# Routing in two groups of 13 and 11 tiles, expert 0 in two chunks, and logits of three tiles side by side: a WKV attention with a mixture of experts on one core

## The chip, the core and the metric

The kernel runs on one core of one Trainium2 chip. The metric is the time of one execution in device microseconds. Three runs of the kernel before gave 615.57 to 617.15, with a median of 616.31 us. The profile shows one further execution; it has five engines: PE (TensorE, with PEld for its weight loads), DVE (VectorE), ACT (ScalarE), POOL (GpSimd) and SP (SyncE, which here issues most of the DMAs).

## The reference

A linear attention with decay (WKV) over 4 batches of 8 heads with 768 tokens of 48 dimensions, then a mixture of 8 experts over its 3072 rows of 384 values. Each row goes to the two experts with the largest noisy logits.

```python
# r, k, v: [4, 8, 768, 48]; w, u: [8, 48]
for t in range(S):
    kt, vt, rt = (k[:, :, t], v[:, :, t], r[:, :, t])
    cur = np.einsum('bhd,bhe->bhde', u[None] * kt, vt)
    y[:, :, t] = np.einsum('bhd,bhde->bhe', rt, state + cur)
    state = w[None, :, :, None] * state + np.einsum('bhd,bhe->bhde', kt, vt)
...
x = np.ascontiguousarray(attn_out.transpose(0, 2, 1, 3)).reshape(B * S, H * D)
...
logits = x @ w_gate                              # [3072, 8]
noise_scale = np.log1p(np.exp(x @ w_noise))
noisy_logits = logits + noise_scale * noise
top2 = np.argpartition(-noisy_logits, 2, axis=1)[:, :2]
...
for e in range(E):
    for k in range(2):
        mask = top2[:, k] == e
        ...
        h = np.maximum(x[mask] @ w1[e], 0.0)     # w1: [8, 384, 1024]
        out[mask] += top2_w[mask, k, None] * (h @ w2[e])
```

## The kernel before

The order of the work is written out by hand: the instructions of each engine run in the order in which the code emits them.

*Attention.* The 24 steps of the loop `for i in range(NT)` take a tile of 128 tokens each. In the trace a step is, on PE: four transposes of r (`trans(i+1, 0)`, L394), the logits of tile i-2 (L497), four transposes of k, kvup (L422, the product of keys and values for the state), inter (L447, the part of y from the state, in four quarters of the array), intra (L459, the part of y within the tile), the scores of the next tile (L406), three transposes of x(i-1) (L485) and four of y (L468). DVE makes rT from the transposed r (L399), the masked scores am (L413), the sum x of a tile (L473), and c (L377), a reduction of the product rku of r, k and u that POOL makes four times with a multiplication and once with an addition (L372). cv (L381), c times v, is on DVE up to tile 9 and on ACT (L388) after that. The decayed state z is two operations on DVE and POOL (L432, L433). SP loads r, k and v four tiles ahead, and weights of expert 0 (`w_load`, L316) into staging buffers; between them it stores each x to the DRAM tensor `xd` (L477), from which the experts gather their rows. DVE and ACT split the loaded weights into a high and a low part (L337, L332).

*Routing.* The logits of a tile are three matmuls with the transposed x as weights and the gate's columns, repeated six times, as the moving side. The tiles are routed in GROUPS of 9, 7 and 8. When a group's logits are there, its generator `route` joins a queue, and `rstep(us)`, called at fixed places of the loop, emits as many of its DVE operations as fit into that many us. They compute the noise scale and the noisy logits for the whole group (elements are tiles x 8 experts), MAX8 and its search for each tile (L709, L715), the two gates, one-hot choices om, a rank for each token by matmuls with a triangle of ones (L739), and with `drop` a list of the rows of an expert by matmuls of two factors r_oa and r_ob (L594). `one(g, 1)` is that list for expert 1, and `half` for the rest. GR (L787) holds the rows to gather. `GEARLY` is the number of groups that the first gather waits for: with groups 0 and 1 (16 tiles) routed, the first EARLY = 512 rows of expert 0 are sure.

*Experts.* Expert e is done in chunks of 128-row tiles; tile 6 has 64 rows. `xgather` issues an indirect DMA per tile on POOL (L954). `xT` transposes a gathered tile on PE (ptm, L1016), ACT copies it (xh, L1018) and DVE makes its low part (xl, L1019). `p1` (L1040) is the first product, 72 matmuls of the chunk's width in eight f of nine, with its eviction on ACT and DVE (L1042, L1044); `p2` (L1074, and L1065 and L1067 for the half tile) the second, 24 matmuls of 384 columns per tile. The result is weighted and scattered into `out` by POOL (L1095). Before that, `out` is zeroed in 16 stores of 288 KB (`zero_out`, SP, L1232), issued while the first chunk runs. Expert 0 has three chunks of 2, 2 and 3.5 tiles, the others two.

## Time and profile before

| | |
|---|---|
| median of three runs | 616.31 us (615.57 to 617.15) |
| the profiled execution | 620.86 us, its span 619.0 us |
| PE busy | 583.0 us (94% of the span) |
| PEld busy | 550.1 us (89%) |
| DVE busy | 375.8 us (61%) |
| ACT busy | 241.9 us (39%) |
| POOL busy | 278.7 us (45%) |
| TensorE's mean granted clock | 0.991 of full speed |
| DMA | 86.03 MB, mean 139 GB/s |

The profiled execution is 4.55 us longer than the median, and 1.86 us of its time lie outside the span. A row of a timeline gives the start and the duration of a run of like instructions; matmuls are pipelined, so a group's pitch (start to start) is what counts and its duration is somewhat longer. Where an engine stood idle before a row, the time and what ended it stand in brackets. On PE, fp32 matmuls are shown in two passes, so the counts in the trace are twice those in the code.

### The profile page before, as it was taken

Reading aid. Unit: us, or ns where it says so; the run is one execution under the profiler, and the core shown is the slowest. Engines: PE = TensorE matmul, PEld = TensorE weight load, DVE = VectorE, ACT = ScalarE, POOL = GpSimd, SP = SyncE. Lnnn points to the kernel's source line nnn. Section 1 sums busy time; section 2 is a strip of 40 time slices with the busy share of each in tenths; the row PEclk is TensorE's granted clock in tenths of the full one; section 3 lists DMA queues with packets and bytes.
Section 4 is the critical chain, followed back from the end, with each engine's and each line's share of the span. In section 5 each row is a group of like instructions: output and inputs, shape, how many; then the busy total and the mean of one; then the engine's idle time right before and its main releaser. Section 6 shows DMA issues by size and latency. Waiting matters only on the chain.

```text
span 619.0 us, 12834 instructions
## 1 busy us (share of the span) xinstructions
PE 583.0 (94%) x4566; PEld 550.1 (89%) x4567; DVE 375.8 (61%) x1006; ACT 241.9 (39%) x596; POOL 278.7 (45%) x428
## 2 busy tenths in 40 slices
...
GB/s 130 184 207 154 192 159 99 171 112 34 177 209 138 142 113 196 75 177 98 225 102 169 144 156 156 116 211 109 158 136 162 138 123 182 133 160 119 40 23 30
DMA packets 134556, 86.03 MB, mean 139 GB/s; under 512 B 109953, under 2 KB 124609, under 8 KB 134482
## 3 DMA queue, kind: packets, MB, share of 16 engines
...
q14 instruction: 36, 0.29, 0.2%
...
## 4 chain that ended last, share of the span: by engine, by line
PE 77%; DVE 10%; DMA 3%; SPq 2%; issue 2%; ACT 1%; another core or an unknown queue 1%; POOL 0%; POOLq 0%; DVEq 0%; ACTq 0%
PE ph L1040 32%; PE pym L1074 31%; PE pa L406 3%; DMA xd<-x 2%; DVE am L413 2%; SPq L135 2%; PE yt L459 1%; PE pym L1065 1%; PE pym L1067 1%; PE pl L497 1%; PE pt L394 1%; PE ptx L485 1%; PE ptb L468 1%; DVE rT L399 1%
## 5 line engine op out<-in xcount | busy, mean ns | idle before, releaser
L1074 PE MATMUL pym<-w1h,hb 128*128 128x384 f32 x768 | 200.2, 337 | 0.9 <-ACT hb L1042 0.7
L1074 PEld LDWEIGHTS pym<-w1h,hb 128*128 128x128 f32 x768 | 138.9, 188 | 3.8 <-issue 2.0
L1040 PE MATMUL ph<-xh,w0h 128*128 128x384 f32 (+3 forms) x408 | 138.2, 339 | 1.5 <-issue 0.9
L1040 PE MATMUL ph<-xl,w0h 128*128 128x384 f32 (+3 forms) x408 | 137.2, 336 | 0.0
L1040 PE MATMUL ph<-xh,w0l 128*128 128x384 f32 (+3 forms) x408 | 136.9, 336 | 0.0
L1044 DVE SCALAR_TENSOR_TENSOR hb<-ph,hb 128x384 fp32r<-128x384 f32 (+1 forms) x136 | 72.4, 533 | 102.2 <-ACT hb L1042 52.5
L1074 PE MATMUL pym<-w1l,hb 128*128 128x384 f32 x384 | 129.2, 337 | 0.4 <-issue 0.4
L1095 POOL DMA_INDIRECT out_dram<-ot,TK x54 | 54.7, 1013 | 151.9 <-DVE ot L1091 122.7
L1042 ACT ACTIVATE hb<-ph 128x384 fp32r<-128x384 f32 (+1 forms) x136 | 64.3, 473 | 111.7 <-PE ph L1040 82.7
L1040 PEld LDWEIGHTS ph<-xh,w0h 128*128 128x128 f32 x408 | 76.6, 188 | 4.0 <-issue 1.1
L1040 PEld LDWEIGHTS ph<-xh,w0l 128*128 128x128 f32 x408 | 76.7, 188 | 1.8
L1040 PEld LDWEIGHTS ph<-xl,w0h 128*128 128x128 f32 x408 | 76.6, 188 | 1.5
L954 POOL DMA_INDIRECT xgt<-xd,GR x40 | 40.4, 1011 | 73.3 <-DMA xq<-xgt 26.6
L1074 PEld LDWEIGHTS pym<-w1l,hb 128*128 128x128 f32 x384 | 72.1, 188 | 0.9 <-issue 0.7
L963 POOL DMA_INDIRECT pv<-out_dram,GA x47 | 51.4, 1093 | 26.4 <-issue 15.0
L1080 ACT ACTIVATE ot<-pym 128x384 f32<-128x384 f32 x39 | 19.2, 492 | 87.2 <-PE pym L1074 68.5
L1019 DVE TENSOR_TENSOR xl<-xq,xh 128x384 fp32r<-128x384 f32 (+1 forms) x40 | 21.5, 539 | 38.1 <-ACT xh L1018 25.2
L413 DVE TENSOR_TENSOR am<-pa,mneg 128x512 int32<-128x512 int32 x48 | 32.7, 683 | 14.5 <-PE pa L406 14.5
L406 PE MATMUL pa<-rT,kT 64*128 64x128 f32 x384 | 27.9, 284 | 10.3 <-DVE rT L399 8.1
L406 PEld LDWEIGHTS pa<-rT,kT 64*128 64x128 f32 x384 | 23.6, 187 | 15.1 <-issue 9.6
L954 POOL DMA_INDIRECT xg<-xd,GR x14 | 14.0, 998 | 48.7 <-DVE f L796 33.5
L362 POOL TENSOR_TENSOR kd<-kt,tabk 128x192 f32<-128x192 f32 x46 | 30.3, 680 | 9.2 <-DMA kt<-in_k_dram 8.6
...
## 6 DMA issues: line engine op xcount, KB each, us to landing
...
xq<-xgt SPq DMA_DIRECT2D x160, 36.0 KB
...
```

Of the source, the lines that this page charges most:

```text
L362: (eng or nc.gpsimd).tensor_mul(kd[i % 3][:, h, :D], kt[i][:, h], tabk[:, h, :D])
L406: nc.tensor.matmul(pa[s][:, p, :], kT[i][s * 64:(s + 1) * 64, p, :], rT[i][s * 64:(s + 1) * 64, p, :], start=True, stop=True)
L413: nc.vector.tensor_tensor(AM[i][:, s].bitcast(I32), PA[i][s].bitcast(I32), mneg.to_broadcast([128, NP, 128]), op=ALU.bitwise_and)
L954: nc.gpsimd.indirect_dma_start(out=xg[:n], out_offset=None, in_=xd[:GROUPS[GEARLY - 1][1] * 128] if early_ else xd, in_offset=bass.Indirec ...
L963: nc.gpsimd.indirect_dma_start(out=pv[:n], out_offset=None, in_=out, in_offset=bass.IndirectOffsetOnAxis(ap=GA[:n, e * NJ + t:e * NJ + t + ...
L1019: nc.vector.tensor_sub(xl[:, g], v, xh[:, g].bitcast(F32))
L1040: nc.tensor.matmul(ph[:, :w_], a[:, d, fs], x[:, :w_ // 32, d], start=(j == 0), stop=(j == len(q) - 1))
L1042: nc.scalar.activation(h_[:, f, 0, :], ph[:, a:b], AF.Relu)
L1044: nc.vector.scalar_tensor_tensor(h_[:, f, 1, :], ph[:, a:b], 0.0, h_[:, f, 0, :].bitcast(F32), op0=ALU.max, op1=ALU.subtract)
L1074: nc.tensor.matmul(py, hb[:, f, a, hs], x[:, f, :], start=(j == 0), stop=(j == len(q) - 1))
L1080: nc.scalar.activation(ot, py, AF.Copy, **({} if e else dict(scale=GT[:, t:t + 1])))
L1095: st = nc.gpsimd.indirect_dma_start(out=out, out_offset=bass.IndirectOffsetOnAxis(ap=TK[:n, q:q + 1], axis=0), in_=ot[:n], in_offset=None, ...
```

## The change

What it does, by engine and place:

- Routing in two groups of 13 and 11 tiles instead of 9, 7 and 8. The first gather now waits for the first 13 tiles and takes 3 tiles of expert 0 (EARLY = 384) instead of 4. The second group is routed during expert 0's first chunk, and expert 1's lists of the first groups, which were made in the attention loop, are made in expert 0's second chunk.
- Expert 0 runs in two chunks of 3 and 3.5 tiles.
- Logits: the transposed x of three tiles are kept (xT has three buffers), and then 9 matmuls put the gate's columns (padded to 32) as weights at three column positions of the array, with 128 columns of x moving. The result has 16 rows for each tile; ACT copies it (ys), PE transposes it back and ACT copies the three tiles' logits at once (`logits_b`, behind kvup).
- Top two: a maximum over the group's 8 columns, compared and weighted with a falling index to pick the first of equals, once more with the winner pushed down by BIG; 13 operations a group.
- For tiles up to 13, POOL's addition in rku is left out (DVE's c reduces 384 elements instead of 192) and the decay's second product is on DVE. cv is on ACT from tile 2 on. rT stands ahead of c in DVE's queue.
- The steps of the loop leave DVE's slots other lengths (STEPS_*, two lines of the table below). The zero row doubles as the source of the warming matmuls; a weight load for expert 1 moves from the second chunk of expert 0 into its first.

The lines left out are the moves of scratch tiles and the renumbered chunks.

```diff
@@ -25,25 +25,25 @@
-STEPS_A = (2.0, 2.2)
+STEPS_A = 1.3
 CV_AT = 5
-STEPS_KV = 0.4
+STEPS_KV = 0.35
...
-STEPS_P1 = 0.75
-STEPS_P2 = 3.9
+STEPS_P1 = 0.85
+STEPS_P2 = 1.1
...
-LREP = 6
-X02_AT = (4, 4, 5, 5)
+CV_DVE = 1
+POOL_LATE = 13
+BIG = 3.0e38
...
@@ -77,19 +77,19 @@
-    CHUNKS0 = ((0, 1), (2, 3), (4, 5, 6))
     CHUNKS1 = ((0, 1, 2), (3, 4, 5, 6))
     CHUNKS2 = ((0, 1, 2), (3, 4, 5))
...
-    EARLY = 512
+    EARLY = 384
...
-    GROUPS = ((0, 9), (9, 16), (16, 24))
-    GEARLY = 2
+    GROUPS = ((0, 13), (13, 24))
+    GEARLY = 1
+    LB = 3
     GB = max(b - a for a, b in GROUPS)
...
@@ -369,19 +367,20 @@
-        nc.gpsimd.tensor_add(rku[:, :, :D // 2], rku[:, :, :D // 2], rku[:, :, D // 2:])
+        if i > POOL_LATE:
+            nc.gpsimd.tensor_add(rku[:, :, :D // 2], rku[:, :, :D // 2], rku[:, :, D // 2:])
...
-        nc.vector.tensor_reduce(c8, RKU[i][:, :, :D // 2], AX.X, ALU.add)
+        nc.vector.tensor_reduce(c8, RKU[i][:, :, :D // 2 if i > POOL_LATE else D], AX.X, ALU.add)
         C8[i] = c8
-        if i <= GROUPS[0][1]:
+        if i <= CV_DVE:
...
     def uterm_c(i, a, b):
-        if i > GROUPS[0][1]:
+        if i > CV_DVE:
...
@@ -430,7 +429,7 @@
             zt = att.tile([128, NP, D], F32, name="zt", bufs=1)
             nc.vector.tensor_add(zt, kvp, Z[b][:, :, :D])
-            nc.gpsimd.tensor_mul(Z[b][:, :, :D], zt, wv)
+            (nc.gpsimd if i > POOL_LATE else nc.vector).tensor_mul(Z[b][:, :, :D], zt, wv)
...
@@ -483,29 +482,46 @@
-        t = att_pool[0].tile([128, ND, 128], F32, name="xT", bufs=1)
+        t = att_pool[0].tile([128, ND, 128], F32, name="xT", bufs=LB)
         nc.scalar.activation(t, pt, AF.Copy)
...
     def logits(i):
         g = [i >= a for a, _ in GROUPS].count(True) - 1
         j = i - GROUPS[g][0]
         if j == 0:
             LG[g] = att_pool[0].tile([128, GB, 2 * E], F32, name="lg")
-        pl = psum.tile([128, LREP, 2 * E], F32, name="pl", tag="py0")
+        if j % LB < LB - 1 and i + 1 < GROUPS[g][1]:
+            return
+        m = j % LB + 1
+        pl = psum.tile([128, 2, 128], F32, name="pl", tag="py0")
         for d in range(ND):
-            nc.tensor.matmul(pl, XT[i][:, d, :], wg[:, d, None, :].to_broadcast([128, LREP, 2 * E]),
-                             start=(d == 0), stop=(d == ND - 1))
-        nc.scalar.activation(LG[g][:, j, :], pl[:, 0, :], AF.Copy)
-
+            for a in range(m):
+                nc.tensor.matmul(pl[32 * a:32 * a + 32, 0, :], wg[:, d, :], XT[i - m + 1 + a][:, d, :],
+                                 start=(d == 0), stop=(d == ND - 1), skip_group_check=True)
+        ys = att_pool[0].tile([128, 128], F32, name="ys", bufs=1)
+        nc.scalar.activation(ys[:32 * m], pl[:32 * m, 0, :], AF.Copy)
+        PL[i] = pl, ys, m
+
+    def logits_b(i):
+        if i not in PL:
+            return
+        pl, ys, m = PL.pop(i)
+        g = [i >= a for a, _ in GROUPS].count(True) - 1
+        j = i - GROUPS[g][0]
+        nc.tensor.transpose(pl[:, 1, :32 * m], ys[:32 * m], ident[:32 * m, :32 * m])
+        nc.scalar.activation(LG[g][:, j - m + 1:j + 1, :],
+                             pl[:, 1, :32 * m].rearrange("p (a b) -> p a b", b=32)[:, :, :2 * E], AF.Copy)
...
@@ -698,30 +713,38 @@
-        yield
-        m8 = T("m8")
-        i8 = T("i8", dt=U32)
-        for j in range(n):
-            nc.vector.max(out=m8[:, j, :], in_=nl[:, j, :])
-            if j % 2:
-                yield
-        da, e2 = P(0, (128, n)) if inp else T("da", [128, n]), T("e2", [128, n])
-        nc.vector.tensor_sub(da, m8[:, :, 0], m8[:, :, 1])
-        for j in range(n):
-            nc.vector.max_index(out=i8[:, j, :], in_max=m8[:, j, :], in_values=nl[:, j, :])
-            yield 0.24
-        nc.vector.tensor_scalar(da, da, 87.0, None, op0=ALU.min)
-        ex = expneg(da, [128, n], "r2", e2, (lambda k: P(k, (128, n))) if inp else None)
-        next(ex)
...
-        nc.vector.tensor_tensor(oh, i8[:, :, 0:2].rearrange("p j k -> p k j")[:, :, :, None].to_broadcast([128, 2, n, E]),
-                                ieu[:, None, None, :].to_broadcast([128, 2, n, E]), op=ALU.is_equal)
+        mx, tb = T("mx", [128, 2, n, 1]), ier[:, None, :].to_broadcast(sh)
+        for kk in range(2):
+            nc.vector.tensor_reduce(mx[:, kk], nl, AX.X, ALU.max)
+            yield
+            q1, ix = P(1 + kk), P(2 - 2 * kk)[:, :, 0:1]
+            nc.vector.tensor_tensor(q1, nl, mx[:, kk].to_broadcast(sh), op=ALU.is_equal)
+            yield
+            nc.vector.tensor_mul(q1, q1, tb)
+            yield
+            nc.vector.tensor_reduce(ix, q1, AX.X, ALU.max)
+            yield
+            nc.vector.tensor_tensor(oh[:, kk], tb, ix.to_broadcast(sh), op=ALU.is_equal)
+            yield
+            if kk == 0:
+                n2 = P(1)
+                nc.vector.scalar_tensor_tensor(n2, oh[:, 0], -BIG, nl, op0=ALU.mult, op1=ALU.add)
+                nl = n2
+                yield
+        da, e2 = P(0, (128, n)), T("e2", [128, n])
+        nc.vector.tensor_sub(da, mx[:, 0, :, 0], mx[:, 1, :, 0])
+        yield
+        nc.vector.tensor_scalar(da, da, 87.0, None, op0=ALU.min)
+        ex = expneg(da, [128, n], "r2", e2, lambda k: P(k, (128, n)))
+        next(ex)
+        yield
...
@@ -1151,40 +1173,36 @@
     def early():
         rows(0, EARLY // 128)
         xgather(0, 0, True)
-        xgather(0, 1, True)
...
     def route_when_done(i):
         for g, (a, b) in enumerate(GROUPS):
             if b == i + 1:
-                while g == GEARLY and route_q:
-                    rstep(1)
                 push(route(g))
-                if g == 0:
-                    push(one(0, 1))
...
         if nxt:
+            trans(i + 1, 0)
             uterm_b(i + 1)
-            trans(i + 1, 0)
         if i > 1:
             logits(i - 2)
-            route_when_done(i - 2)
         if nxt:
             trans(i + 1, 1)
         kvup(i)
+        if i > 1:
+            logits_b(i - 2)
+            route_when_done(i - 2)
         inter(i)
...
-        rstep(STEPS_A[i > GROUPS[1][1]], False)
+        rstep(STEPS_A, False)
...
             early()
-            push(one(1, 1))
...
@@ -1223,8 +1241,9 @@
     xtrans(NT - 1)
     next(p1a)
     logits(NT - 1)
+    next(p1a)
+    logits_b(NT - 1)
     route_when_done(NT - 1)
-    gap[0] = 2
...
@@ -1234,37 +1253,37 @@
     for j, _ in enumerate(p1a):
-        if j == XT_AT_0:
-            for _ in xT(0, 1):
-                pass
         zero_out()
         rstep(STEPS_P1)
-    for t in p2(0, 0, zero_out):
+
+    done = [False]
+
+    def routes_done():
+        if not route_q and not done[0]:
+            done[0] = True
+            rows(EARLY // 128, NJ)
+            xgather(0, 1)
+            tokens(0, NJ)
+
+    def step00():
+        zero_out()
         rstep(STEPS_P2)
+        routes_done()
+
+    wl = w_p2(0, 0)
+    next(wl)
+    for t in p2(0, 0, step00):
+        next(wl, None)
         hold.append((0, t))
...
     while route_q:
         rstep(1)
-    if not done:
-        routes_done()
+    routes_done()
```

How this moves the instructions is shown at three places. In the names, am is the masked scores, x the tile's output, c the reduced rku, z the state.

On DVE, step 1 of attention, before:

```order
L377 TENSOR_REDUCE c_361<-rku 128x8
L381 TENSOR_TENSOR cv<-vd_92,c_361 128x384
L399 TENSOR_TENSOR rT<-pt,pwr 128x512
L435 TENSOR_TENSOR z_187<-pwarm,w_159 128x4x48
L413 TENSOR_TENSOR am<-pa,mneg 128x512
L473 TENSOR_TENSOR x<-ptb,cv 128x384
```

and now:

```order
L398 TENSOR_TENSOR rT<-pt,pwr 128x512
L376 TENSOR_REDUCE c_362<-rku 128x8
L434 TENSOR_TENSOR z_188<-pwarm,w_160 128x4x48
L412 TENSOR_TENSOR am<-pa,mneg 128x512
L472 TENSOR_TENSOR x<-ptb,cv 128x384
```

rT, which the next scores on PE wait for, moved ahead of c, and cv left DVE.

On PE, from the scores of attention's step 6 to intra of step 7, before (pl is the logits, pt the transposes of r and k, pwarm kvup, yt inter and intra):

```order
L406 MATMUL pa<-rT,kT 128x128 x8
L485 MATMUL ptx<-ident,x 128x128 x3
L468 MATMUL ptb<-ident,yb 128x128 x4
L394 MATMUL pt<-ident,rd_86 128x128 x4
L497 MATMUL pl<-wg,xT 128x96 x3
L394 MATMUL pt<-ident,kd_85 128x128 x4
L422 MATMUL pwarm<-vd_93,kd_84 48x48 x8
L447 MATMUL yt<-rT,z_189 64x128 x8
L459 MATMUL yt<-am,vd_93 64x128 x8
```

and now, from the same scores:

```order
L405 MATMUL pa<-rT,kT 128x128 x8
L484 MATMUL ptx<-ident,x 128x128 x3
L467 MATMUL ptb<-ident,yb 128x128 x4
L393 MATMUL pt<-ident,rd_86 128x128 x4
L502 MATMUL pl<-xT,wg 32x128 x9
L393 MATMUL pt<-ident,kd_85 128x128 x4
L421 MATMUL pwarm<-vd_93,kd_84 48x48 x8
L514 MATMUL pl<-ident,ys 128x96
L446 MATMUL yt<-rT,z_190 64x128 x8
L458 MATMUL yt<-am,vd_93 64x128 x8
```

Every third step has nine matmuls of logits and, between kvup and inter, the transpose of their copy ys; the other steps have neither.

On PE, the transposes ptm of expert 0's second chunk, before, in the middle of the first chunk's first product:

```order
L1040 MATMUL ph<-xh,w0h_711 128x256
L1040 MATMUL ph<-xl,w0h_711 128x256
L1040 MATMUL ph<-xh,w0l_712 128x256
L1016 MATMUL ptm<-ident,xg 128x128 x6
L1040 MATMUL ph<-xh,w0h_711 128x256
```

and now, at the end of the first chunk's second product:

```order
L610 LDWEIGHTS r_oa
L610 MATMUL pwarm<-r_ob,r_oa 128x14
L1039 MATMUL ptm<-ident,xg 128x128 x9
L1039 MATMUL ptm<-ident,xg 128x64 x3
L1063 MATMUL ph<-xh,w0h_728 128x448
L1063 MATMUL ph<-xl,w0h_728 128x448
L1063 MATMUL ph<-xh,w0l_729 128x448
```

They stand directly behind the last list matmuls (L610), and the first product of the second chunk follows on them.

## Rows read from the trace of the kernel before

**Rows 1.** The page, part 4: shares of the chain that ended last, by engine.

```profile
PE 77%; DVE 10%; DMA 3%; SPq 2%; issue 2%; ACT 1%; another core or an unknown queue 1%; POOL 0%; POOLq 0%; DVEq 0%; ACTq 0%
```

**Rows 2.** Timeline of PE: start, us, operation, tiles, shapes, count [idle before <-releaser].

```profile
160.72 0.37 PE L1040 MATMUL ph<-xh,w0h 128*128 128x256 f32 x1
...
228.21 0.34 PE L1040 MATMUL ph<-xh,w0h 128*128 128x384 f32 x1
...
229.08 0.33 PE L1040 MATMUL ph<-xh,w0l 128*128 128x384 f32 x1
...
257.89 0.36 PE L1040 MATMUL ph<-xh,w0h 128*128 128x448 f32 x1
```

**Rows 3.** Windows: bounds, length, each engine busy (count), PEclk, DMA share, GB/s.

```profile
12.00:14.00 2.00, 2.00 (x25) 1.67 (x25) 0.17 (x1) 0.60 (x1) 2.00 (x4) 0.50 1.35 180
...
30.00:40.00 10.00, 10.00 (x151) 8.84 (x150) 6.43 (x14) 4.03 (x11) 9.15 (x16) 1.00 1.05 224
...
258.00:608.00 350.00, 349.53 (x1951) 341.74 (x1950) 175.28 (x347) 129.59 (x268) 131.05 (x169) 1.00 0.50 137
```

**Rows 4.** Timeline of DVE: x of steps 9, 13 and 22.

```profile
72.82 0.56 DVE L473 TENSOR_TENSOR x<-ptb,cv 128x384 f32<-128x384 f32 x1 [1.47 <-DMA xd<-x]
...
99.55 0.56 DVE L473 TENSOR_TENSOR x<-ptb,cv 128x384 f32<-128x384 f32 x1 [0.28 <-PE ptb L468]
...
155.48 0.56 DVE L473 TENSOR_TENSOR x<-ptb,cv 128x384 f32<-128x384 f32 x1 [0.23 <-PE ptb L468]
```

**Rows 5.** Timeline of DVE: the reduction c of tile 1.

```profile
14.97 0.35 DVE L377 TENSOR_REDUCE c<-rku 128x8 f32<-128x192 f32 x1 [2.80 <-POOL rku L372]
```

**Rows 6.** Timeline of PE: first transposes, scores of tiles 1 and 2.

```profile
11.40 1.09 PE L394 MATMUL pt<-ident,rd 128*128 128x128 f32 x4 [2.22 <-DMA rd<-in_r_dram]
...
17.00 1.16 PE L406 MATMUL pa<-rT,kT 64*128 64x128 f32 x16 [1.72 <-DVE rT L399]
...
21.94 1.16 PE L406 MATMUL pa<-rT,kT 64*128 64x128 f32 x16 [0.93 <-DVE rT L399]
```

**Rows 7.** Timeline of PE: parts of steps 12 and 13 of attention.

```profile
88.48 0.56 PE L422 MATMUL pwarm<-vd,kd 128*48 128x48 f32 x16
88.97 0.67 PE L447 MATMUL yt<-rT,z 48*64 48x128 f32 x16
89.57 1.09 PE L459 MATMUL yt<-am,vd 128*64 128x128 f32 x16
...
93.18 0.60 PE L468 MATMUL ptb<-ident,yb 128*128 128x128 f32 x4
...
94.06 0.84 PE L497 MATMUL pl<-wg,xT 128*128 128x96 f32 x6
94.74 0.60 PE L394 MATMUL pt<-ident,kd 128*128 128x128 f32 x4
```

**Rows 8.** Timeline of DVE: routing of group 0 in steps 11 and 12.

```profile
86.03 1.02 DVE L699 SCALAR_TENSOR_TENSOR r_q<-r_q,prt 128x72 f32<-128x72 f32 x4
...
88.83 0.68 DVE L413 TENSOR_TENSOR am<-pa,mneg 128x512 int32<-128x512 int32 x1
89.43 1.00 DVE L337 TENSOR_TENSOR w1l<-stg,w1h 128x768 fp32r<-128x768 f32 x1
90.35 0.36 DVE L709 MAX8 r_m<-r_nl 128x8 f32<-128x8 f32 x4
```

**Rows 9.** Timeline of DVE and POOL: GR, first and last early gather.

```profile
152.79 0.17 DVE L787 TENSOR_SCALAR GR<-lt 128x4 int32<-128x4 f32 x1
...
153.25 1.16 POOL L954 DMA_INDIRECT xg<-xd,GR  x1 [7.63 <-DMA xd<-x]
...
157.24 0.95 POOL L954 DMA_INDIRECT xg<-xd,GR  x1 [0.30 <-issue]
```

**Rows 10.** Windows (as rows 3), behind the last scatter.

```profile
612.00:613.00 1.00, 0.00 (x0) 0.00 (x0) 0.00 (x0) 0.00 (x0) 0.00 (x0) 0.50 0.05 15
```

**Rows 11.** Timeline of POOL: the last scatter of the kernel.

```profile
609.59 0.98 POOL L1095 DMA_INDIRECT out_dram<-ot,TK  x1 [3.10 <-DVE ot L1091]
```

119 lines of the change are left out of this document (48 added, 71 removed).

## The prediction

> **What bounds the kernel now.** I read the chain of the work that ended last first: TensorE has 77% of it and VectorE 10% [rows 1], so every step has to be costed on TensorE, with VectorE second. The rows of TensorE in the experts' part then give three marks [rows 2]: the first expert matmul of expert 0 starts at 160.72, expert 1's first chunk at 228.21, its second chunk at 257.89. From 258 to 608 TensorE is busy 349.53 of 350 us [rows 3], and the change leaves that stretch as it is. So the change is worth as much as it moves 257.89. I cut what lies before it into attention (to 160.72), expert 0 (67.49 us to 228.21) and the first chunk of expert 1 (29.68 us, same work before and after).
>
> In attention the start of x, the output of a step's tile, marks the pace [rows 4]. Steps 0 to 5 wait in two places. VectorE stands 2.80 us for GpSimd's rku before the reduction c of tile 1 [rows 5], and because c and cv stand ahead of rT in its queue, TensorE's scores wait for rT: 1.72 and 0.93 us in the first two steps [rows 6], and little after. The DMA engines are full there, too: a share of 1.05 from 30 to 40 us [rows 3]. Steps 5 to 9 are a loop through SyncE: the store of x stands behind a weight load that waits for its staging buffer, and x of the next step but one waits for that store to land (VectorE stands 1.47 us for it ahead of x of step 9 [rows 4]). From x of step 9 to that of step 22 it is 82.66 us (72.82 to 155.48), and there VectorE is full: the routing of the first two groups lies between its attention work without a gap [rows 8]. TensorE's own work of a step is far smaller. From the rows of one step [rows 7]: kvup 0.49 (88.48 to 88.97), inter 0.60 (88.97 to 89.57), intra 1.02 (1.09 less the 0.07 by which such a group outlasts its pitch), eight transposes 0.88 (93.18 to 94.06), so 0.44 for four and 0.38 for the three of x with a start, logits 0.68 (94.06 to 94.74), and 1.09 for the scores, whose group is 1.16 [rows 6]. That is 5.6 us with logits and 4.9 without.
>
> **Attention, part by part.** *Start.* The scores of tile 1 now wait neither for c nor cv, since rT stands first. The transposes that rT needs are done by about 14; what is left is rT after the other work of TensorE, so the scores start at about 15.3 instead of 17.00: 1.7 us. The wait of 0.93 goes as well: 2.6, and a little more with the small ones behind it. The reductions over 384 instead of 192 elements (about +0.2 each) and the decay product on VectorE (+0.3, by the 0.35 of c over 192 elements [rows 5]) are covered by the cv, an operation over 384 elements, that moves to ScalarE. The DMA engines being full to 40 us, I take 3.2 us at most at step 9 and nothing more from steps 5 to 9, whose loop through SyncE the change does not touch. Bounds: 0 (the loads set the pace and the loop swallows the gain) and 4.2.
>
> *Steps 9 to 13.* Group 0's routing starts only after 13 tiles, so VectorE has here only its attention work: two masks, the low part of a weight, x, c, rT and the two of the decay, some 4.2 us a step by my estimate. TensorE sets the pace: 4.9 plus a little, say 5.0, and one step of three has the new logits. Their price is the first unknown. 9 matmuls are 18 passes. If the three column tiles run one after another, a pass costs the 0.113 us of today's logits pass (0.68 over 6 [rows 7]): 2.03. If they run side by side as well as the four tiles of inter do (0.0375 a pass), 0.68. Nearest is intra, which has two column tiles and the same 128 columns, at 0.064 a pass; for three tiles I scale to 0.042 and take 0.75. To this come the transpose back (0.11) and the wait for ScalarE's copy ahead of it: inter waits behind it, and there is 0.93 us of other work to cover a copy that queues behind kT's 0.6; I take 0.45, from 0 to 0.9. Together 1.3 us in steps 10, 13, 14, 17, 20. Steps 9 to 13 then take 4 x 5.0 + 2 x 1.3 + 0.3 = 22.9 instead of 26.73 us (72.82 to 99.55): 3.8 won.
>
> The Trainium skill speaks against this piece: TensorEngine Tiling (Array Packing), section Key Properties, says that a change of the tiling mode (not just of the tile) drains TensorE. Here kvup, inter and intra follow each other at their plain pitch [rows 7], so this trace shows no drain to speak of. By that rule two more changes a piece, each at most the 0.16 us by which a group of logits outlasts its pitch (0.84 less 0.68), would cost 0.3 x 5 = 1.6 us, and the forecast would be 615.0.
>
> *Steps 13 to 22.* Routing of 13 tiles goes into VectorE's slots of steps 14 to 22. Its operations are 104 elements instead of 72; four of 72 take 1.02 us [rows 8]. The top two now are 13 operations on the whole group, where each tile had MAX8 (four in 0.36) [rows 8] and a search that I take for a little longer: 24 tiles at 0.24 are 5.8 us, the new ones at about 0.22 are 2 x 2.9: neutral. What VectorE wins is one group's worth of fixed overhead, the two list passes of expert 1, and cv. Step by step I get 7.1, 6.0, 5.2, 6.3, 5.2, 7.3, 6.2, 4.5, 5.1 = 52.9 instead of 55.93 (99.55 to 155.48): 3.0. At x of step 22 the gain is 3.2 + 3.8 + 3.0 = 10.0. From there to the first expert matmul it was 5.24; with one more tile to transpose and copy I take 5.6. Expert 0 starts 9.7 us earlier, at P = 151.0.
>
> **Expert 0.** The chunks of 3 and 3.5 tiles need the second list before the second chunk, where the old chunks of 2, 2 and 3.5 had a chunk in between. The chain, from P, is this. The evictions of the first chunk and the head of group 1's routing share VectorE to P+15.7. Behind the last eviction stand some 21 operations of 88 elements at 0.27 and five small ones: the choice om is there at P+22.4, while TensorE reaches the rank matmuls (after 40 of the 72 matmuls of the second product, at 0.174 each: 5 lie between 228.21 and 229.08 [rows 2]) at P+20.9. So it stands 1.5 us there. Then 0.5 for the ranks, and 32 more matmuls to P+28.5. Meanwhile VectorE runs slots, gates, the two wide comparisons (1.7) and the list factors: 5.9 us, ready at P+29.1. The list matmuls end at P+29.6. Three small operations lead to GR, each like GR's own 0.17 [rows 9], 0.6 in all, and the gather of 153.25 was issued 0.29 us after GR's end; so the first of four gathers starts at P+30.5. Four starts span 3.99 us (153.25 to 157.24) and thus the last starts at P+34.3. How long a gather takes to land no row shows by itself. The last scatter of the kernel starts at 609.59 [rows 11], and its bytes have all but stopped by 612 [rows 10]: 2.4. I take 2.7, as there are four in a row, from 2.0 to 5 (six of the zero stores, 1.8 MB at 224 GB/s [rows 3], 7.9 us, may still be under way since they stand right behind the gates' store). With the transpose, the copy and the low part (1.2) the second chunk starts at P+38.2. TensorE stands still for 8.6 us less its own transposes, and that is the price of this part of the change. Nothing else can fill the gap, since the order has only transposes and then the 448 wide matmuls.
>
> The rest has fewer, wider matmuls. The second chunk takes 15.2 for its first product (72 matmuls of 448 columns, at 448/384 of 0.174, are 14.6; 0.6 for list work), and 15.25 for its second (72 matmuls at 0.174 and 16 of the half tile), with 0.85 of transposes, 0.45 of list matmuls and about 2.4 us of waits for VectorE's lists; some 0.4 is left over. So expert 1 starts at P+72.8 instead of P+67.49: 5.3 lost. The third chunk, which used to cover the list work, is gone, and so is the time that its narrow matmuls took; both are in these sums.
>
> *The clock.* After 2.22 us without work ahead of 11.40 [rows 6], early in attention, the granted clock was 0.50 from 12 to 14 [rows 3], so at least 2 us of work ran at 1.2 GHz; after the last matmul, short of 609, it is 0.50 from 612 on [rows 10]. A stall of over 8 us will do the same. Two us at half speed cost 1.0; I take 3 us and 1.5. Bounds: 0 and 3.
>
> **The sum.** 9.7 won, 5.3 and 1.5 lost: 2.9. The second chunk of expert 1 starts at 255.0 instead of 257.89, the span goes from 619.0 to 616.1 and the profiled execution from 620.86 to 618.0. That one lies 4.55 over the median of 616.31; the difference is carried over unchanged, which gives 613.4.
>
> **The rivals.** *A, slower: the column tiles run one after another.* Each logits piece then costs 2.03 instead of 0.75, in five steps in which TensorE sets the pace: 6.4 us, 619.8. For it: all three write one accumulator bank with three sets of weights. Against it: inter's tiles do run side by side. The sign turns where a piece costs 0.58 us more than I took, at 1.33.
> *B, the second list is later than I have it.* Each us by which om, the list factors or the gathers come later goes to the end in full. Six zero stores ahead of the gathers, or VectorE still busy with evictions, make 3 to 4 us: 617. From a stall of 11.5 us on the gain is gone.
> *C, the early gain is swallowed.* If x of step 9 stays at 72.8 because the loads and the loop through SyncE set it, 3.2 us are missing: 616.6. The share of 1.05 speaks for it, the waits for rT against.
> *D, more is won.* Steps 14 to 22 at TensorE's pace (3 us), gathers that land after 2.0 us (0.7) and a clock that doesn't fall (1.5) make 608.2.
>
> **How the numbers follow.** Forecast 0.45, A 0.12, B 0.15, C 0.13, D 0.15. The likeliest is 613.4, its own range 610.5 to 616. To hold 8 of 10, the range goes to 606.5 (most of D) and 619 (B, C and the edge of A). About 0.3%, 1.85 us, is what a measurement can tell from no change. Faster than 614.46: most of the forecast (0.36), D (0.15), a little of the others: 0.53. Slower than 618.16: A and the upper half of B, 0.21. The rest is 0.26.
>
> **What would show it.** x of step 9 near 69.5, of step 13 near 92.4, of step 22 near 145.3, the first expert matmul near 151.0. The group of logits matmuls at 0.75 and not 2.0. One wait of 8 to 9 us on TensorE ahead of the transposes for the second chunk near 180 to 189, with a granted clock of 0.50 behind it. Expert 1 near 224 to 225. If the wait is over 12 us, or x of step 22 not before 150, the forecast is wrong.

## The result and the profile after

The changed kernel takes 624.87 us, the median of four runs (623.82 to 625.98), beside 616.53 for the kernel before in the same comparison: a ratio of 1.0147 with an interval of 1.0124 to 1.0171. It is slower by 8.3 us; 613.4 was forecast, with a range to 619.0. The profiled execution of after takes 624.16 us, its span 622.4.

On the page of after, part 4 (the chain that ended last, by engine), TensorE's share falls from 77% [rows 1] to 73%, and waits on DMA and on ScalarE grow:

```profile
PE 73%; DVE 10%; issue 6%; DMA 5%; ACT 4%; POOL 1%; SPq 1%; POOLq 0%; DVEq 0%; ACTq 0%
```

Attention came close to the forecast. The timeline of VectorE in after (start, us, operation, shapes, idle before) has x of steps 9, 13 and 22 at 69.4, 93.5 and 146.0, where [rows 4] have 72.82, 99.55 and 155.48; forecast were 69.5, 92.4 and 145.3:

```profile
69.36 0.56 DVE L472 TENSOR_TENSOR x<-ptb,cv 128x384 f32<-128x384 f32 x1 [0.86 <-DMA xd<-x]
...
93.52 0.56 DVE L472 TENSOR_TENSOR x<-ptb,cv 128x384 f32<-128x384 f32 x1 [0.29 <-ACT xT L486]
...
146.02 0.56 DVE L472 TENSOR_TENSOR x<-ptb,cv 128x384 f32<-128x384 f32 x1 [0.29 <-PE ptb L467]
```

Behind it time is lost. The timeline of TensorE in after, from the last logits piece of the attention loop to the first expert matmul:

```profile
146.15 0.86 PE L502 MATMUL pl<-xT,wg 128*32 128x128 f32 x18 [0.23 <-ACT xT L486]
147.39 0.30 PE L514 MATMUL pl<-ident,ys 96*128 96x96 f32 x1 [0.38 <-ACT ys L505]
147.99 0.67 PE L446 MATMUL yt<-rT,z 48*64 48x128 f32 x16 [0.30 <-ACT lg L515]
...
150.31 0.90 PE L1039 MATMUL ptm<-ident,xg 128*128 128x128 f32 x3 [0.84 <-DVE xl L1042]
151.14 1.98 PE L458 MATMUL yt<-am,vd 128*64 128x128 f32 x16
...
153.59 0.42 PE L1063 MATMUL ph<-xh,w0h 128*128 128x384 f32 x1
```

The transpose of ys, inter and the last gathered tile each stand for a copy, and intra takes 1.98 us instead of 1.09 [rows 7], at a granted clock that had fallen (columns as [rows 3]: each engine's busy time, then granted clock, DMA share, GB/s); nopack, a run below without the packed logits, keeps 1.00 from 149 to 151.

```profile
150.00:152.00 2.00, 1.69 (x11) 1.36 (x13) 0.95 (x3) 0.81 (x4) 0.00 (x0) 0.54 0.00 0
```

Expert 0 starts at P = 153.6 instead of 151.0.

Then the stall. TensorE in after, from the ranks of the second group (L760) over its list (L610) to the second chunk of expert 0, and GpSimd's four gathers for that chunk:

```profile
177.37 0.20 PE L760 MATMUL pwarm<-r_om,ltri 128*128 128x88 bf16 x1 [1.80 <-DVE r_om L751]
...
183.87 0.42 PE L610 MATMUL pwarm<-r_ob,r_oa 128*128 128x14 bf16 x11 [0.35 <-DVE r_ob L606]
190.19 0.90 PE L1039 MATMUL ptm<-ident,xg 128*128 128x128 f32 x3 [5.91 <-DMA xg<-xd,GR]
192.00 0.90 PE L1039 MATMUL ptm<-ident,xg 128*128 128x128 f32 x3 [0.90 <-DMA xg<-xd,GR]
193.35 1.38 PE L1039 MATMUL ptm<-ident,xg 128*128 128x128 f32 x6 [0.45 <-DMA xg<-xd,GR]
195.16 0.74 PE L1063 MATMUL ph<-xh,w0h 128*128 128x448 f32 x1 [0.42 <-ACT xh L1041]
...
196.20 0.58 PE L1063 MATMUL ph<-xh,w0l 128*128 128x448 f32 x1
196.58 0.57 PE L1063 MATMUL ph<-xh,w0h 128*128 128x448 f32 x1
```

```profile
185.16 0.94 POOL L977 DMA_INDIRECT xg<-xd,GR  x1 [37.68 <-DVE f L819]
...
188.90 0.91 POOL L977 DMA_INDIRECT xg<-xd,GR  x1 [0.30 <-issue]
```

The first gather starts at 185.16, and the transposes that need its rows at 190.19, 5.0 us later. SyncE's queue shows what moves at that time: six stores of 288 KB of zeros.

```profile
180.88 0.40 SPq L790 DMA_DIRECT2D xd<-r_a  x1
...
182.04 5.59 SPq L1251 DMA_DIRECT2D out_dram<-zrow  x6
```

The windows of after there show full DMA engines in the stall, and a clock of 0.50, 1.2 GHz, up to 6 us into the second chunk:

```profile
185.00:188.00 3.00, 0.00 (x0) 0.00 (x0) 0.99 (x7) 0.00 (x0) 2.23 (x3) 0.95 1.04 376
188.00:195.00 7.00, 3.19 (x12) 1.90 (x12) 1.33 (x3) 1.90 (x8) 2.52 (x4) 0.50 0.60 201
195.00:201.00 6.00, 5.84 (x15) 5.08 (x16) 1.81 (x8) 1.74 (x5) 2.20 (x5) 0.50 0.26 98
201.00:202.00 1.00, 1.00 (x5) 0.91 (x5) 1.00 (x3) 0.00 (x0) 0.00 (x0) 0.81 0.00 0
```

Expert 1's two chunks start at 234.31 and 262.93, where [rows 2] have 228.21 and 257.89:

```profile
234.31 0.33 PE L1063 MATMUL ph<-xh,w0h 128*128 128x384 f32 x1
...
262.93 0.36 PE L1063 MATMUL ph<-xh,w0h 128*128 128x448 f32 x1
```

### The profile page after: what moved, and what is told of

It is laid out like the page before. It is cut to its first block, busy times and chain, and to the rows that moved or that the text cites. A ratio compares the mean times of both kernels' runs of the same rounds, so it can differ in the third digit from the quotient of the medians.

```text
span 622.4 us, 12573 instructions
## 1 busy us (share of the span) xinstructions
PE 583.9 (94%) x4502; PEld 544.9 (88%) x4503; DVE 363.8 (58%) x856; ACT 252.4 (41%) x646; POOL 265.3 (43%) x403
## 4 chain that ended last, share of the span: by engine, by line
PE 73%; DVE 10%; issue 6%; DMA 5%; ACT 4%; POOL 1%; SPq 1%; POOLq 0%; DVEq 0%; ACTq 0%
PE ph L1063 31%; PE pym L1097 29%; ACT cv L387 2%; DMA xd<-x 2%; DVE am L412 2%; PE yt L458 1%; PE ptx L484 1%; DMA xg<-xd,GR 1%; PE pym L1090 1%; PE pym L1088 1%; PE pa L405 1%; PE pt L393 1%; PE ptb L467 1%; DVE rT L398 1%; DMA kt<-in_k_dram 1%
## 5 line engine op out<-in xcount | busy, mean ns | idle before, releaser
L1063 PE MATMUL ph<-xh,w0h 128*128 128x384 f32 (+1 forms) x384 | 135.6, 353 | 0.4 <-ACT xh L1041 0.4
L1063 PE MATMUL ph<-xl,w0h 128*128 128x384 f32 (+1 forms) x384 | 134.6, 351 | 0.0
L1063 PE MATMUL ph<-xh,w0l 128*128 128x384 f32 (+1 forms) x384 | 133.9, 349 | 0.0
L1067 DVE SCALAR_TENSOR_TENSOR hb<-ph,hb 128x384 fp32r<-128x384 f32 x128 | 71.2, 557 | 103.5 <-ACT hb L1065 54.0
L1065 ACT ACTIVATE hb<-ph 128x384 fp32r<-128x384 f32 x128 | 62.9, 492 | 109.4 <-PE ph L1063 107.7
L1063 PEld LDWEIGHTS ph<-xh,w0h 128*128 128x128 f32 x384 | 73.0, 190 | 3.4 <-ACT xh L1041 0.6
L1063 PEld LDWEIGHTS ph<-xh,w0l 128*128 128x128 f32 x384 | 73.0, 190 | 2.3
L1063 PEld LDWEIGHTS ph<-xl,w0h 128*128 128x128 f32 x384 | 72.9, 190 | 2.2 <-DVE xl L1042 0.2
L387 ACT ACTIVATE cv<-vd,c 128x48 f32<-128x48 f32 x176 | 44.2, 323 | 24.3 <-DVE c L376 22.5
L1041 ACT ACTIVATE xh<-xq 128x384 fp32r<-128x384 f32 (+1 forms) x40 | 20.2, 506 | 32.6 <-DVE xq L1031 29.2
```

The costliest lines, as they stand in the source:

```text
L387: nc.scalar.activation(CV[i][:, h, :], vt[i][:, h, :], AF.Copy, scale=C8[i][:, h, :])
L1041: nc.scalar.activation(xh[:, g], v, AF.Copy)
L1063: nc.tensor.matmul(ph[:, :w_], a[:, d, fs], x[:, :w_ // 32, d], start=(j == 0), stop=(j == len(q) - 1))
L1065: nc.scalar.activation(h_[:, f, 0, :], ph[:, a:b], AF.Relu)
L1067: nc.vector.scalar_tensor_tensor(h_[:, f, 1, :], ph[:, a:b], 0.0, h_[:, f, 0, :].bitcast(F32), op0=ALU.max, op1=ALU.subtract)
```

## The experiments

Theory 1: the gain of attention is real, and expert 0 in two chunks eats it, as its stall is longer than forecast (gathers beside the zero stores, the clock behind). Rivals: the attention edits or the packing cost time by themselves; the loss belongs to single waits elsewhere. The five sessions differ in speed (the kernel before took 614.9 to 625.2 us, and in the second and the fourth, both on chip 11, 624.7 and 615.6), so each ratio is against runs of the kernel before in its own session.

| kernel | ratio to before | interval |
|---|---|---|
| before_again / before_trace | 1.0006 / 1.0008 | 0.9988–1.0023 / 0.999–1.0025 |
| att_only / att_cv / att_nopack | 1.011 / 1.014 / 1.0034 | 1.0067–1.0154 / 1.0072–1.0209 / 1.0–1.0067 |
| pack_only / pack_again / pack_tail | 1.011 / 1.0058 / 1.0052 | 1.0068–1.0152 / 1.0036–1.008 / 1.003–1.0075 |
| nopack / nopack_zf | 1.0102 / 1.0033 | 1.0071–1.0133 / 0.9997–1.0069 |
| fill / zero_early / zero_fill | 1.0122 / 1.0103 / 1.011 | 1.0083–1.0161 / 1.0073–1.0133 / 1.0071–1.0149 |
| after_again / cv_dve / late_ptm / combo | 1.0189 / 1.0237 / 1.0188 / 1.0113 | 1.013–1.0247 / 1.0176–1.0298 / 1.0122–1.0254 / 1.0051–1.0176 |
| no_wait | 1.017 | 1.0105–1.0236 |

before_again, att_only, fill and zero_early are of one session; after_again, cv_dve, late_ptm and combo of the next; no_wait, zero_fill, att_cv and pack_only of the third; before_trace, pack_again, pack_tail and nopack of the fourth; nopack_zf and att_nopack of the fifth.

**The kernel before, traced again.** No edit.

> The kernel before, unchanged, for a second trace of it. Theory 1 (the one trace of before is 4.5 us longer than its timed runs): time 616.5, a span of 614 to 615, expert 1's second chunk starts at about 253.5 and not at 257.89, and some of the waits in the first trace are missing. Rival (spans always lie that far over the timed runs): the same rows again, second chunk at 257.9.

> The unchanged kernel, for a trace on the same chip as the three that follow. Theory 1 (packing costs its time through its own copies and waits): the marks of this trace are the base; first expert matmul at 160 to 164, expert 1's first chunk 65.5 to 67.5 us later, its second 27.6 to 29.7 us after that. Rival (the lost time of the packed kernels sits in waits of the experts that this chip shows whatever the kernel): expert 1's first chunk 68 us or more after the first, as in the packed kernels on such a chip, and the second 31 us after it. Time 613 to 627 us, depending on the chip.

The first profiled execution again was 3.6 us above its median of 615.0. The second was not (616.12, median 616.26), and its marks on TensorE are the better base:

```profile
161.30 0.36 PE L1040 MATMUL ph<-xh,w0h 128*128 128x256 f32 x1
...
226.35 0.34 PE L1040 MATMUL ph<-xh,w0h 128*128 128x384 f32 x1
...
254.00 0.36 PE L1040 MATMUL ph<-xh,w0h 128*128 128x448 f32 x1
```

Expert 0 takes 65.05 us here (65.38 in before_again) and not the 67.49 of [rows 2], and expert 1's first chunk 27.65 in both and not 29.68. Windows of TensorE say why. The trace ahead of the prediction:

```profile
202.00:216.00 14.00, 12.48 (x89) 11.88 (x88) 11.54 (x32) 7.82 (x21) 5.92 (x10) 1.00 0.45 148
240.00:258.00 18.00, 16.91 (x107) 15.34 (x106) 11.62 (x39) 2.74 (x8) 6.75 (x8) 1.00 0.53 128
```

and before_trace over the same work:

```profile
202.00:214.00 12.00, 12.00 (x89) 11.90 (x88) 11.76 (x37) 7.55 (x20) 7.26 (x11) 1.00 0.60 180
239.00:254.00 15.00, 15.00 (x101) 14.37 (x100) 10.55 (x37) 2.39 (x8) 7.07 (x9) 1.00 0.56 134
```

In the first TensorE idles 1.5 and 1.1 us over work that it does without a gap in the second (a busy time is modelled and takes in part of a wait). By the marks, 2.4 and 2.0 us of that execution were waits of its own, in the very stretch that the change moves. In slower sessions expert 1's first chunk is longer, too, whatever the kernel: 29.6 us in att_nopack and 33.5 in after_again.

**The attention edits alone**, in the kernel before with its three groups and chunks: packing, rT first, cv and GpSimd's work as in the change (att_only); with cv on VectorE up to tile 9 as of old (att_cv); with the old logits (att_nopack).

```diff
-CV_DVE = 1      # att_only
+CV_DVE = 9      # att_cv
```

> The kernel before with the attention edits alone: logits of three tiles side by side, rT ahead of c, cv on ScalarE from tile 2, the addition and the decay on VectorE up to tile 13; groups of 9, 7 and 8, MAX8, three chunks of expert 0 and their order stay. Theory 1 (the attention edits win, all of the loss lies in expert 0's two chunks and the wait for the second list): 610 to 613, x of step 9 near 69.4, the first expert matmul 4 to 6 us earlier than before. Rival (with the routing of two groups still in steps 10 to 22 VectorE sets the pace there and swallows the gain): 616 to 617.

> The kernel before with the attention edits, but cv on VectorE up to tile 9 as before (CV_DVE = 9). Theory 1 (cv on ScalarE stands ahead of the eviction yb and waits for c, which now stands behind rT; TensorE waits for yb): x of step 9 at 70.5 to 72 and not 73.4, and 0.3 to 0.7% faster than the attention edits with cv on ScalarE. Rival (the groups' routing on VectorE in steps 10 to 22 is what loses the 5 us): x of step 9 earlier, but the same end within 0.2%.

> The kernel before with its groups of 9, 7 and 8 and three chunks, with rT ahead of c, cv on ScalarE from tile 2 on and GpSimd's addition and decay left out up to tile 13; logits as before. Theory (in the old routing VectorE sets the pace of steps 9 to 22, so what these edits win early is given back there): within 0.6% of before on either side, x of the first tile 2 to 4 us earlier than in the kernel before, x of step 22 not more than 2 us earlier. Rival (the edits pay by themselves and only the packing spoilt them in the kernel with both): faster than before by 0.4% or more.

Nothing is won by any, and x of step 9, expected near 69.4 in att_only, comes at 73.4. In att_nopack x of step 0 comes at 16.4 and x of step 22 at 159.5; in before_trace, of another session, at 20.0 and 156.9. The window of att_only from 80 to 100 shows the bound: VectorE busy 19.14 us of 20 (fifth column: 9.21 for ScalarE), as in before_trace with 19.31. In after it is 13.93, since no routing lies there. The gain of attention needs the new groups; without them VectorE takes the early gain back: from x of step 9 to that of step 22 it is 87.4 us in att_nopack and 82.8 in before_trace. A part was gone before: at step 9 the lead is down from 3.5 to 1.9 us, with waits of 1.0 to 2.1 us for the store of x in steps 4 to 9, the loop of rival C. Nor did cv on VectorE help: att_cv, expected 0.3 to 0.7% faster than att_only, is at 1.014.

```profile
80.00:100.00 20.00, 15.14 (x218) 12.20 (x217) 19.14 (x72) 9.21 (x33) 13.13 (x21) 0.91 0.70 132
```

```profile
80.00:100.00 20.00, 18.64 (x273) 15.47 (x274) 13.93 (x35) 12.88 (x45) 11.23 (x20) 1.00 0.66 140
```

(att_only above, after below.)

**The packing alone**, in the kernel before (pack_only, and again as pack_again beside before_trace); the same with old logits in the last group (pack_tail); and the change without it (nopack).

```diff
+        if g == len(GROUPS) - 1:          # pack_tail: one tile at a time, as before
+            pl = psum.tile([128, LREP, 2 * E], F32, name="pl", tag="py0")
...
+            return
```

> The kernel before with the logits of three tiles side by side alone; order of rT and c, POOL's addition, the decay and cv as before. Theory 1 (TensorE is not what bounds steps 10 to 22 with this routing, and inter now waits 0.3 us for the logits' copy in every third step): within 0.4% of before, rather slower. Rival (TensorE's 0.45 us less a step is won): 0.8 to 1.3% faster.

> The kernel before with the logits of three tiles side by side and nothing else, once more, beside a trace of the kernel before on the same chip. Theory 1: 1.0 to 1.2% over before, and against before's trace the first expert matmul is not earlier although x of step 22 is, since the time from x of step 22 to it has grown by 2 us or more (7.7 against 5.3). Rival: within 0.4% of before on this chip.

> As the last, but the eight tiles of the last group have the old logits, so the last steps of attention have neither the copy ys nor the transpose back. Theory 1 (the chain of logits, copy, transpose, copy ahead of inter is what costs, and above all in the last steps where nothing covers it): about half of the loss is back, 0.3 to 0.7% over before; from x of step 22 to the first expert matmul 5.2 to 6 us. Rival (the loss does not come from that chain): as slow as the last kernel, 1.0% or more over before.

> The changed kernel with the old logits (six repeats, one tile at a time); groups of 13 and 11 and two chunks of expert 0 stay. Theory 1 (the packing costs about 1% by itself): 0.3 to 0.8% over before instead of 1.4 to 1.9, with x of step 13 near 92 to 94 and x of step 22 near 146. Rival (packing is neutral or helps in the new routing, where TensorE sets the pace of steps 9 to 13, and the two chunks alone are the loss): 1.4 to 1.9% over before, or more, x of step 13 near 94 to 95.

Packing costs 0.6% where before takes 615.6 us, and 1.1% where it takes 625.2. Half of my account of it fell: from x of step 22 to P it is 4.8 us in pack_again and 4.4 in before_trace, so the bare chain costs no 2 us there, and taking it out of the last group gives back nothing (1.0052). In pack_again's profile all marks lie 0.6 to 0.7 us behind those of before_trace. But that execution, at a mean clock of 0.993, is the quickest of its six, 617.08; the four of 0.977 to 0.986 take 618.7 to 620.2, while the kernel before has 0.985 to 0.990 in its ten. The profile of pack_tail caught such a case. Windows of before_trace and of pack_tail, 80 to 100: 245 matmul records in both, at clocks of 1.00 and 0.83, and 16.36 against 18.30 us for them.

```profile
80.00:100.00 20.00, 16.36 (x245) 13.89 (x245) 19.31 (x79) 11.17 (x39) 14.69 (x24) 1.00 0.76 151
```

```profile
80.00:100.00 20.00, 18.30 (x245) 15.19 (x246) 17.99 (x73) 10.04 (x36) 16.07 (x27) 0.83 0.73 139
```

That the packed kernel, with less matmul work to bridge the waits for VectorE, loses the clock more often would fit both, but is not shown; what makes it fall in one execution and not in another, and why the loss doubles in the slower session, stays open. Without packing, the change still loses 1.02%, some two thirds of its loss; by the marks of nopack against before_trace attention wins 10.3 us there and expert 0 loses 14.9. In nopack P is 151.00, to the digit the forecast, which is luck: the forecast had the packed logits in it, and in nopack_zf, without them too, P is 152.95 in a slower session.

```profile
151.00 0.43 PE L1051 MATMUL ph<-xh,w0h 128*128 128x384 f32 x1
...
230.94 0.33 PE L1051 MATMUL ph<-xh,w0h 128*128 128x384 f32 x1
```

**The stall taken apart**, in the changed kernel: 28 matmuls on zeros in it (fill); the zero stores four at a time, ahead of the gathers (zero_early); both (zero_fill, 22 matmuls); both without packing (nopack_zf).

```diff
+    for _ in range(FILL):                 # fill, behind the list matmuls
+        nc.tensor.matmul(pfill, wsrc[:, :128], wsrc, start=True, stop=True)
...
-        zero_out()                        # zero_early
+        for _ in range(4):
+            zero_out()
```

> The changed kernel with 28 matmuls of zeros (bf16, 512 columns, into an accumulator that nothing reads) on TensorE between the last list matmul of group 1 and the transposes of expert 0's second chunk, about 6 us of its wait. Theory 1 (the wait costs twice: itself, and the granted clock of 0.50 behind it, under which the next 6.4 us of work run at half pace): 3 to 4 us faster than the changed kernel, 621, clock 1.00 from 184 to 200. Rival (the clock falls for the waits between the transposes anyway, or the time is set by the gathers alone): 624 to 625.

> The changed kernel with the 16 zero stores of the output issued four per step of expert 0's first product, so that all stand ahead of the store of group 1's gates and none runs beside the gathers of the second chunk. Theory 1 (six zero stores of 288 KB, with the DMA engines at a share of 1.0 from 185 to 192, delay the gathers): first transposes 3 us after the gather's start and not 5, wait on TensorE 1.5 to 2 us shorter, 622.5 to 623.5. Rival (a gather takes 4 to 5 us to land by itself): 624.9.

> The changed kernel with two of the edits together: zero stores issued early and 22 matmuls of zeros in the wait (4.7 us). Theory 1 (the two prices of the wait, its length and the clock, are separate): the second chunk starts 38 to 39 us behind the first, at a clock of 1.00, expert 1 at 72 to 74 us and not 80.7; 0.3% slower than before to even. Rival (the clock falls for the short waits between the transposes anyway): as the early zero stores alone, 75.7 us and 1.0% slower.

> The changed kernel with the old logits, with all zero stores issued early and 22 matmuls on zeros in the stall of expert 0. Theory (packing, the zero stores beside the gathers and the clock behind the stall are shares of the loss that add up, and the rest is the bare wait for the second list): 1.0% over before less 0.4 to 0.5% for the zero stores, less 0 to 0.3% for the zeros: 0.2 to 0.7% over before; second chunk of expert 0 at 38.5 to 41 us behind the first, expert 1 at 75 to 78 behind it. Rival (the shares don't add; each of these edits only shows what the next wait hides): 0.8 to 1.2% over before.

zero_early: the first transposes come 3.1 us behind the first gather, not 5.0, and the later ones wait less. TensorE of zero_early:

```profile
187.78 0.90 PE L1039 MATMUL ptm<-ident,xg 128*128 128x128 f32 x3 [3.97 <-DMA xg<-xd,GR]
189.06 0.90 PE L1039 MATMUL ptm<-ident,xg 128*128 128x128 f32 x3 [0.37 <-DMA xg<-xd,GR]
...
192.46 0.74 PE L1063 MATMUL ph<-xh,w0h 128*128 128x448 f32 x1 [0.42 <-ACT xh L1041]
```

with the gather that they wait for:

```profile
184.69 0.94 POOL L977 DMA_INDIRECT xg<-xd,GR  x1 [36.48 <-DVE f L819]
```

The second chunk starts at P+39.4 instead of P+41.6, expert 1 at P+75.7 instead of P+80.7. fill leaves the second chunk at P+41.1 and brings expert 1 to P+77.4: the clock in 188 to 195 is 0.94 (after: 0.50), in 195 to 201 still 0.79.

```profile
188.00:195.00 7.00, 4.61 (x22) 2.42 (x21) 1.94 (x4) 2.04 (x8) 2.97 (x5) 0.94 0.60 205
195.00:201.00 6.00, 6.00 (x25) 5.44 (x25) 2.41 (x9) 2.15 (x5) 1.17 (x3) 0.79 0.18 66
```

Not all of this is the edits' doing. From the start of the second chunk to expert 1 it is 39.15 us in after, 36.36 in zero_early and 36.32 in fill, but also 36.20 in after_again, the changed kernel as it is (197.52 to 233.72). Its clock comes back 3.5 us into the chunk and not after 6 (first product 16.80 us, in after 18.05), and does not fall a second time, behind the waits for expert 1's gathers, as it does in after (second product 19.40 and 21.10 us). The waits themselves are in both: 1.29 and 0.61 us, 1.35 and 0.67. The windows of after and of after_again:

```profile
225.00:229.00 4.00, 3.92 (x15) 3.92 (x16) 3.60 (x6) 0.60 (x3) 1.60 (x4) 0.57 0.39 139
```

```profile
225.00:229.00 4.00, 3.39 (x21) 3.15 (x22) 3.90 (x9) 1.16 (x4) 2.52 (x6) 1.00 0.54 184
```

So the stores cost some 2 us of wait. The clock costs up to 3 us in the second chunk, differently from one execution to the next, and that the zeros win any of it is not shown: fill's 1.0122 can't be told from the 1.0147 of the first comparison. In zero_fill the two together give no more than one (1.011 in a slower session, where after_again has 1.0189): there TensorE is at the zeros until 191.90, 3.7 us behind the first gather, and so holds up transposes that came 3.1 us behind it in zero_early. nopack_zf is 1.0033 of before, with an interval that takes in 1; with nopack's 1.0102 the shares add up as expected. Its clock still falls to 0.50, from 193 to 195, and expert 0 takes 75.7 us; that what is left is the bare wait for the list is argued, not shown. None of these beats the kernel before.

**The wait taken away.** no_wait gathers the second chunk's rows early, from the first group's list; those of its rows that the second group would add are wrong.

```diff
-        rows(0, EARLY // 128)
+        rows(0, NJ)
         xgather(0, 0, True)
+        xgather(0, 1, True)
```

> The changed kernel with the gathers of expert 0's second chunk issued right behind the early ones, from the list of the first group as it then stands, so that nothing waits for the second list's gathers; the rows of that chunk past the first group's are then not the chosen ones, and that part of the output is not the reference's. Every other instruction stays, the routing of group 1 and its lists too. Theory 1 (the loss lies in that wait and the granted clock of 0.50 behind it): the second chunk starts 32 to 33 us behind the first and not 41.6, the clock stays at 1.00 there, the kernel is 11 to 13 us faster than the changed one, 0.4 to 0.6% faster than before. Rival (other waits take its place: the second one in the second chunk, VectorE's lists): 0.5 to 1% slower than before.

Expert 0 falls to 72.6 us, by 8; the second chunk starts 36.6 us behind the first, where Theory 1 had 32 to 33. The total, expected 11 to 13 us shorter, doesn't follow: P comes at 159.4, since TensorE stood 4.07 us ahead of the transpose of ys and ran at clocks of 0.58 and 0.50 behind it. ScalarE's copy ys, which that transpose reads, had itself started after 4.65 us of idle time, for which the trace names no engine; the cause stays open. The run shows the price of the wait, not a gain.

**Smaller parts**, in the changed kernel: once more (after_again); cv on VectorE up to tile 13 (cv_dve); expert 1's first transposes 24 matmuls later (late_ptm); these two with zero_early and 18 matmuls on zeros (combo).

```diff
-CV_DVE = 1
+CV_DVE = 13                               # cv_dve, combo
...
-                for _ in range(2):        # late_ptm, combo
-                    next(xt, None)
+                if listed[0] is not True:
+                    for _ in range(2):
+                        next(xt, None)
+                listed[0] = 2
```

> The changed kernel, unchanged, beside the experiments on one chip. Theory 1 (the +8.3 us is the kernel, not the chip): 1.1 to 1.7% over before. Rival (a part of it is a single disturbed chip): under 1%.

> The changed kernel with cv on VectorE up to tile 13 as one operation (CV_DVE = 13 instead of 1), on ScalarE after that. Theory 1 (in steps 1 to 13 the eight cv operations on ScalarE wait for c and stand ahead of the eviction yb, so that TensorE waits 0.5 to 1.1 us a step for yb): those waits go, steps 9 to 13 take 21.5 to 23 us instead of 24.2, x of step 13 is 1.5 to 3 us earlier, and so is the end. Rival (VectorE has no room for 0.9 us more, or the loads set the pace): x of step 13 at 93.5 or later.

> The changed kernel with the transposes of expert 1's first two tiles one output tile (24 matmuls, 4.2 us) later in expert 0's second chunk, so that their gathers have landed. Theory 1 (this is the second wait of the change: 1.35 and 0.67 us for the gathers, some 1.5 us between them, and a granted clock of 0.50 from 225.4 to 228.3): expert 1 starts 2.5 to 3.5 us earlier and the kernel is as much faster. Rival (the wait only moves to the other end, since the last transposes then stand just ahead of expert 1): under 1 us.

> The changed kernel with all four: zero stores issued early, 18 matmuls of zeros in the wait, cv on VectorE up to tile 13, the later transposes for expert 1. Theory 1 (the four costs are separate and add up: 5 for the zero stores' and the wait's clock together with the fill, 2 for cv, 3 for the transposes): 613 to 615 where before is 615 and the changed kernel 623. Rival (they overlap in the same waits): 617 to 619.

after_again loses 1.89%, more than the 1.1 to 1.7 expected, in a session where the kernel before takes 624.7. Beside it cv_dve takes steps 9 to 13 from 24.1 to 22.8 us and loses 1.0 in the steps before; late_ptm changes nothing from expert 0's second chunk to expert 1 (36.4 against 36.2), as its waits only move to the end of the chunk, 1.18 and 0.58 us ahead of expert 1. Only combo gains, by what zero_early has.

## Right and wrong, step by step

| us | rows 2 | before_trace | forecast | after | nopack |
|---|---|---|---|---|---|
| to the first expert matmul, P | 160.72 | 161.30 | 151.0 | 153.59 | 151.00 |
| expert 0 | 67.49 | 65.05 | 72.8 + 1.5 | 80.72 | 79.94 |
| expert 1, first chunk | 29.68 | 27.65 | 29.68 | 28.62 | 28.64 |
| from there to the span's end | 361.1 | 360.4 | 361.1 | 359.5 | 359.6 |
| span | 619.0 | 614.4 | 616.1 | 622.4 | 619.2 |

From before_trace to after it is 7.7 won, 15.7 and 1.0 lost and 0.9 won: 8.0 us, beside the measured 8.3. From the forecast 613.4 to 624.87 it is 11.5: three steps of the prediction make 14.3 of it, and the two stretches behind, shorter by 1.1 and 1.6, take 2.7 off.

*The difference carried over unchanged: 5.3 us.* The forecast took 4.55 us off, because the profiled execution lay so far above the median; after's own profile lies 0.7 below its median. Of those 4.5 us, 2.4 sat in expert 0 as waits of that one execution, and my chunk lengths for expert 0 in after, built from pitches, had no such waits: these were taken off twice. The 2.0 in expert 1's first chunk I had kept (29.68), so they were taken off once, rightly; the 2.7 by which the stretches behind came out shorter about cancels them and the 0.7. By the same parts against before_trace, expert 0 would have lost 9.2 against 65.05, and the change would have stood about even, near 615.8. This alone takes the forecast from faster to no change.

*Expert 0: 6.4 us.* The chain to the second list was right within 1.1 us: TensorE waited 1.80 for om (forecast 1.5), the first gather started at P+31.6 (P+30.5). The landing was mis-sized: 2.7 from the start of the last gather, where 188.90 to 193.35, the start of the last transposes, is 4.45, and 5.0 for the first gather. Rival B had named the six zero stores and the bound of 5 all but held, yet I took the lower value from a scatter with nothing beside it [rows 10, 11]. So the second chunk started at P+41.6 and not P+38.2: 3.4, of which 1.0 is the chain, 1.8 the landing and 0.6 the transposes and copies behind it, at half the clock. The clock cost about 2.9 and not 1.5: some 17 matmuls of 448 columns at 0.373 us (196.20 to 196.58 and on) instead of 0.203 (448/384 of the 0.174 that the prediction takes from [rows 2]). The rest, 1.6, is the second fall of the clock, behind the waits for the gathers of expert 1, 0.66 or less from 225 to 229, which I had not costed at all. Without it, in after_again, the second product and its waits take 19.40, where my parts make 19.35.

*The end of attention: 2.6 us.* x of step 22 came 0.7 later than forecast, and from there to P it took 7.6 instead of 5.6. The packed logits piece is in step 23 too, where neither the transposes of k nor kvup cover the copies, and the clock fell (0.54 from 150 to 152). nopack, without that piece, takes 5.6: of the 2.0 between them 0.7 lie ahead of inter, at the copies, and 1.3 behind it, where the clock is low. It is 6.3 and 6.4 in fill and zero_early, so a part differs from one execution to the next.

*What held.* The three marks of x, to 0.1, 1.1 and 0.7 us. The 1.1 is the middle: steps 9 to 13 took 24.2 instead of 22.9, as TensorE did not set the pace there but waited for ScalarE's copy yb behind cv (0.68 and 0.74 us at 79.98 and 85.91), and the steps after it made up 0.4. The price of the packed logits: 0.78 us (0.75 forecast) for three tiles side by side, so rival A fell, and with the transpose and its wait 1.39. The step is on TensorE in after, and below it the next step, without logits:

```profile
68.52 0.60 PE L393 MATMUL pt<-ident,rd 128*128 128x128 f32 x4
69.05 0.86 PE L502 MATMUL pl<-xT,wg 128*32 128x128 f32 x18
69.83 0.66 PE L393 MATMUL pt<-ident,kd 128*128 128x128 f32 x4
70.42 0.56 PE L421 MATMUL pwarm<-vd,kd 128*48 128x48 f32 x16
70.91 0.30 PE L514 MATMUL pl<-ident,ys 96*128 96x96 f32 x1
71.52 0.67 PE L446 MATMUL yt<-rT,z 48*64 48x128 f32 x16 [0.30 <-ACT lg L515]
...
75.05 0.60 PE L393 MATMUL pt<-ident,rd 128*128 128x128 f32 x4
75.49 0.60 PE L393 MATMUL pt<-ident,kd 128*128 128x128 f32 x4
76.02 0.57 PE L421 MATMUL pwarm<-vd,kd 128*48 128x48 f32 x16
```

The transposes ahead of the piece and behind it are start to start 0.09 and 0.06 us longer than in the step without logits (0.53 and 0.59, there 0.44 and 0.53), so a piece costs 0.15 us more at its edges, which the sum had left out. The Trainium skill's rule (TensorEngine Tiling (Array Packing), section Key Properties) that a change of the tiling mode drains TensorE would lengthen a piece; the trace shows no more than these 0.15 us, half of the 0.3 that the prediction worked out for it. Rival C fell (x of step 9 at 69.36), D too. The end is rival B's: 10.9 us from the list matmuls' end (184.3) to the second chunk, near the 11.5 at which it had the gain gone; yet at 617 B too was far from 624.87. Neither sign that was to show the forecast wrong came true, a wait over 12 us or x of step 22 not before 150: they left out the base and the clock. One slip without weight: the old third chunk of expert 0 has 2.5 tiles (its matmuls are 320 columns wide), not 3.5.
